# Re-orderings in a fused retention and snake-MLP kernel: a later cast, neighbouring value sets, other engines for squares, a first state and a sum, and swapped PSUM banks

## The chip, the core and the metric

The kernel runs on one core of a Trainium2 chip. The metric is the device time of one execution in microseconds (us); the median of the runs shown is compared. On the core five engines work beside each other, each through its own instruction stream in order: TensorE (PE in the profile, its weight loads PEld), VectorE (DVE), ScalarE (ACT), GpSimd (POOL) and SyncE (SP), which here only issues DMAs. They meet through semaphores: an instruction that waits holds up everything behind it on its own engine.

## The reference

Eight batches of causal retention (8 heads, 576 positions, head size 64), whose output is reshaped to 4608 tokens of 512 and goes through an MLP with a snake activation:

```python
scores = scale * np.matmul(q, k.transpose(0, 1, 3, 2))
Dmat = np.where(rel >= 0, gamma[:, None, None] ** rel[None, :, :], 0.0)
attn = np.matmul(scores * Dmat, v)                 # (8, 8, 576, 64)
x = attn.transpose(0, 2, 1, 3).reshape(8 * 576, 512)
h = x @ w_in                                       # (4608, 2048)
s = np.sin(alpha * h)
out = (h + s * s / (alpha + 1e-9)) @ w_out         # (4608, 512)
```

## The kernel before

**The retention.** The decay is folded into q and k when they are cast from float32 to float16 (`cast`, L138; the multiplication is L181; a v is only copied, by `copy`, L102 on ACT and L104 on DVE or POOL). A batch's first 512 positions are two blocks, `p` 0 and 1, of two chunks `g` each. Per block: `scores` (L348) multiplies k and q into a PSUM tile of two banks, `masked` (L366, the instruction is L370, on DVE) applies the causal mask and makes `ret`, and `values` (L379, matmul L401) multiplies `ret` with v. `outer` (L285, matmul L298) makes the sums of k times v per chunk; `take_sum`, `evict` and `evict_bank` copy them from PSUM to `kvs`; `more` (L336) carries the decayed sum on from chunk to chunk on POOL; `to_state` (L331, the instruction is L332) multiplies a chunk's sum by one decay factor per partition and head (`g1`, four columns) into a float16 state, one POOL instruction of 128x256. `add_states` (L412, matmul L423) adds state times q to the values, and `keep` (L430) casts the result to `xT`, the input of the MLP.

**Two value sets and their order.** The values of a block come in two sets, "not same" and "same", which use different halves of the array's rows on the same PSUM bank, so the second may begin only when the first is through. With `relay=engine` an empty instruction on that engine waits for the first set's last matmul, and the second set's first matmul waits for it (`told`, L248; `order`, L240). It stands in that engine's stream like any other instruction. Without a relay TensorE drains itself before the second set (`change_rows`, L234).

**The MLP.** 512 tokens are a block `n`; the 2048 columns of h are 16 units. `project(n, u, tag)` (L528, four matmuls L536 for all 512 columns, or four for each half) fills the bank `tag`; `sine` (L541, L544, ACT) reads it; `square` (L549; L553 on ACT, L555 on DVE or POOL) squares the sine; `product` (L558, L560, DVE) adds the scaled square to h, writes `gT` and so frees the bank. `gemm2(n, u, tag)` (L577, four matmuls L582) multiplies `gT` with w_out for blocks 0 and 1; `finish` (L571) evicts and stores. From block 2 on the second product is done with seven instead of eight quarter products (`Quarters`, L605): its sums `s1` to `s4` of parts of `gT` (L619 to L631) run on DVE or POOL, its matmuls are L653.

**What sets the order.** All of it is written out by hand: `tc.manual_schedule()` keeps each engine's instructions in the order of the calls. PSUM has eight banks under six names: `h0`, `h1`, `h2`, `op` of one bank, `m0`, `m1` of two. A call that takes a name waits until the last user of that bank has been read. Blocks 0 to 2 of the MLP are interleaved call by call with batches 1 to 4 of the retention; from block 3 on a loop over `n` does it. Loads go out on SP's queue, w_in and w_out on POOL's. Six raw buffers hold loaded q, k and v; a `load` waits until a buffer has been cast.

Around the change, before:

- Batch 0, L785 to L833: POOL casts the second block's q, ACT takes the transposes out of PSUM (`take`), POOL makes the first state (L803), and the second block's two value sets stand with `project(0, 0)` between them (L827 to L829), the relay on DVE.
- Units 0 to 3 of block 0, L840 to L855: squares on DVE, ACT, POOL, DVE.
- Block 1 with batch 2, L1029 to L1113. `at[2].outer` takes `op` and `h2`. On ACT the cast of the second half of batch 3's first v (L1076) stands between `sine(1, 12)` and `square(1, 12)`. The first value sets of both blocks (L1096, L1097) have a relay on DVE, with `product(1, 14)` and a cast behind; `gemm2(1, 4)` stands between first and second sets.
- Block 3, L1414: the sum `Q.s1(1)` on DVE after unit 10.

Of the kernel before, what the change touches and what calls it, by code (L numbers as in the profile page):

```python
# [18 lines left out]
def kernel(  # L19
# [16 lines left out]
    nc = tc.nc  # L36
# [37 lines left out]
    g1 = cn[:, 48:52]  # L74
# [13 lines left out]
    V, A_, G_ = nc.vector, nc.scalar, nc.gpsimd  # L88

    def load_w_in(g):  # L90
        cols = slice(g * 512, (g + 1) * 512)
        nc.gpsimd.dma_start(w_in16[:, :, cols], w_in_r[:, :, cols])
# [161 lines left out]
    class Attention:  # L254
# [76 lines left out]
        def to_state(self, c, eng=None):  # L331
            (eng or nc.gpsimd).tensor_tensor(  # L332
                self.state_of(c), self.kvs[:, c], g1.unsqueeze(2).to_broadcast([P, 4, D]), MULT
            )

        def more(self, c):  # L336
# [212 lines left out]
    def square(n, fc, eng):  # L549
        s_t = hps_of[n, fc][1]  # L550
        ss_t = work.tile([P, 512], F16, tag="ss", bufs=4, name="ss_t")
        if eng is nc.scalar:
            nc.scalar.activation(ss_t, s_t, mybir.ActivationFunctionType.Square)  # L553
        else:
            eng.tensor_tensor(ss_t, s_t, s_t, MULT)  # L555
        hps_of[n, fc][1] = ss_t
# [137 lines left out]
    def keep_busy(n, tag, m=512):  # L694
        idle = psum.tile([P, 512], F32, tag=tag, bufs=1, name="idle")
        for _ in range(n):
            matmul(idle[:, 0:m], zero[:, 0:P], zero[:, 0:m], start=True, stop=True)  # L697
# [43 lines left out]
    with tc.manual_schedule():  # L741
# [44 lines left out]
        cast(0, "q", 1, G_, (1,))  # L786
        load_w_in(2)
        keep_busy(5, "h2", 256)
        turn(0, "q", 1, "op", (0,))
# [12 lines left out]
        keep_busy(4, "h1", 256)  # L802
        at[0].to_state(0, G_)  # L803
        cast(0, "v", 1, G_, (0,))
# [21 lines left out]
        load_w_in(3)  # L826
        at[0].values(1, False, "m0", relay=V)  # L827
        project(0, 0, "op", 0)
        at[0].values(1, True)  # L829
        at[0].add_states(1, (0,))  # L830
        project(0, 1, "h2", 0)
        at[0].add_states(1, (1,))
        at[0].keep(1, A_)  # L833
        project(0, 2, "h0", 0)
        project(0, 3, "h1", 0)
# [7 lines left out]
        sine(0, 1)  # L843
        square(0, 1, A_)
        product(0, 0)
        project(0, 2, "h0", 1)
        sine(0, 2)
        square(0, 2, G_)
        product(0, 1)
        project(0, 3, "h1", 1)  # L850
        sine(0, 3)
        square(0, 3, V)
        product(0, 3)
        project(0, 4, "m1")
        product(0, 2)  # L855
        sine(0, 4)
# [171 lines left out]
        square(1, 6, A_)  # L1028
        at[2].outer((0, 1), "op", "h2")  # L1029
        at[2].evict_bank(1, V)  # L1030
        project(1, 7, "h0", 0)
        project(1, 7, "h0", 1)
        at[2].evict_bank(0, V)
        project(1, 8, "h1", 0)
        project(1, 8, "h1", 1)
        sine(1, 8)
# [8 lines left out]
        product(1, 8)  # L1045
        project(1, 10, "op", 0)
        project(1, 10, "op", 1)
        sine(1, 10)
# [12 lines left out]
        at[2].scores(0, 0, "m0")  # L1061
        gemm2(1, 0, "h1")
        sine(1, 9)
# [9 lines left out]
        project(1, 12, "h0", 1)  # L1073
        gemm2(1, 1, "h1")
        sine(1, 12)
        cast(3, "v", 0, A_, (1,))  # L1076
        square(1, 12, A_)
        product(1, 12)
        cast(3, "q", 1, G_)
        project(1, 13, "op", 0)  # L1080
        project(1, 13, "op", 1)
        gemm2(1, 2, "h1")
        at[2].scores(1, 0, "m0")
# [11 lines left out]
        square(1, 13, A_)  # L1095
        at[2].values(1, False, "m1", relay=V)  # L1096
        at[2].values(0, False, "m0", relay=V)  # L1097
        product(1, 14)
# [7 lines left out]
        cast(3, "q", 0, G_)  # L1106
        gemm2(1, 4, "h2")
        at[2].values(0, True)
# [3 lines left out]
        at[2].add_states(1)  # L1112
        at[2].keep(1, A_)  # L1113
        gemm2(1, 5, "h2")
        project(2, 3, "m0", 0)
# [27 lines left out]
        at[3].scores(1, 0, "m1")  # L1143
        gemm2(1, 3, "h1")
        project(2, 2, "op")
        project(2, 7, "h0")
# [11 lines left out]
        product(2, 7)  # L1158
        project(2, 11, "h1")
        gemm2(1, 12, "h2")  # L1160
# [9 lines left out]
        cast(4, "v", 1, A_)  # L1170
        project(2, 0, "op")
        at[3].masked(0, 1)
# [8 lines left out]
        sine(2, 0)  # L1181
        gemm2(1, 8, "h1")
        gemm2(1, 9, "h1")
        gemm2(1, 10, "h1")
        gemm2(1, 11, "h1")
        sine(2, 4)
        project(2, 8, "h0")
        cast(4, "q", 1, G_, (0,))
        project(2, 6, "op")
        cast(4, "k", 1, G_, (1,))  # L1190
# [4 lines left out]
        finish(1, 2)  # L1195
        at[4].outer((0, 1), "h2", "h1")
        cast(4, "q", 0, G_, (1,))
# [28 lines left out]
        sine(2, 5)  # L1226
        project(2, 15, "h1", 0)
        project(2, 15, "h1", 1)
        sine(2, 15)
# [4 lines left out]
        product(2, 15)  # L1234
        project(2, 13, "op", 0)
        project(2, 13, "op", 1)
        project(2, 14, "m0", 0)
# [42 lines left out]
        for n in range(3, NBLK):  # L1280
# [96 lines left out]
            if n == 3:  # L1377
                for x in KEYS[3:]:
                    cast(n + 2, *x, G_)
            if n == 6:  # L1380
                for j in range(3):
                    last_tokens(j, "cast")
                last_tokens(3, "load")
# [27 lines left out]
            if B2:  # L1411
                crossed(n + 2, 0, "k")
                crossed(n + 2, 1, "k")
            if n == 3:  # L1414
                Q.s1(1, V)
            if n == 8:
# [90 lines left out]
```

## Time and profile before

| | us |
|---|---|
| median of 3 runs | 299.24 |
| lowest, highest | 297.9, 300.09 |
| the profiled execution, its own time | 301.06 |
| its span, first to last instruction | 299.3 |
| TensorE busy in the span | 284.2 (95%) |
| VectorE busy | 220.2 (74%) |
| ScalarE busy | 209.7 (70%) |
| GpSimd busy | 207.1 (69%) |

The granted TensorE clock is 0.99 of full speed in the mean. A line of the timeline gives an instruction's start and duration in us, engine, source line, operation, the tile that it writes and those that it reads, and the count of instructions merged into it; in square brackets stands the idle time of the engine just before, and what ended it.

### The profile page before, as it was taken

How to read it: one execution, taken by the hardware profiler on the slowest of the kernel's cores; microseconds unless marked ns; L12 is line 12 of the kernel's file. 1: busy time of each engine (PE TensorE's matmuls, PEld its weight loads, DVE VectorE, ACT ScalarE, POOL GpSimd, SP SyncE). 2: the span in 40 equal slices, each digit the busy share in tenths (PEclk: the TensorE clock that was granted, in tenths of full speed). 3: DMA queues.
4: the chain of work that ended last, by engine and by line, in shares of the span. 5: the costliest groups of instructions: out<-in, count | busy, mean ns of one | idle time of the engine just before them, and what ended most of it. 6: DMA issues, size and time to landing. Idle time of an engine off the chain costs nothing.

```text
span 299.3 us, 8757 instructions
## 1 busy us (share of the span) xinstructions
PE 284.2 (95%) x3607; PEld 185.1 (62%) x3607; DVE 220.2 (74%) x299; ACT 209.7 (70%) x336; POOL 207.1 (69%) x200
## 2 busy tenths in 40 slices
PE   7798999997699999999999999999999999999993
PEld 5563454575354576666666666766666666665782
DVE  3849977886667899998778767786769485756871
ACT  2659832876376799787878787878777878887600
POOL 4876889999989787988897899779925900370000
PEclk9999999999799999999999999999999999999998
DMA  7999999998989297989699768676747201310225
GB/s 227 288 255 221 271 212 291 230 213 259 244 202 268 55 169 174 236 207 198 153 266 187 161 158 238 76 168 147 159 107 176 55 1 41 70 37 17 62 50 119
DMA packets 119159, 49.89 MB, mean 167 GB/s; under 512 B 69824, under 2 KB 118096, under 8 KB 119120
## 3 DMA queue, kind: packets, MB, share of 16 engines
q1 hardware_dynamic: 114528, 45.04, 64.0%
q0 software_dynamic: 4224, 4.19, 8.5%
q8 instruction: 28, 0.46, 0.7%
q10 hardware_dynamic: 368, 0.11, 0.2%
q14 instruction: 11, 0.09, 0.1%
HBM read 36.74 MB, written 9.44 MB: 154 GB/s over the span
## 4 chain that ended last, share of the span: by engine, by line
PE 82%; POOL 6%; ACT 4%; DVE 3%; DMA 2%; issue 2%; SPq 0%; ACTq 0%; DVEq 0%; POOLq 0%
PE hps L536 35%; PE hps L653 29%; PE ops L582 6%; POOL T L603 3%; PE sc L358 2%; DMA v<-in_v_dram 2%; PE o L401 2%; PE idle L697 2%; PE kv L298 2%; PE tr L215 1%; ACT s_t L544 1%; DVE ret L370 1%; DVE gT L560 1%; PE o L423 1%; POOL kvs L340 1%
## 5 line engine op out<-in xcount | busy, mean ns | idle before, releaser
L560 DVE SCALAR_TENSOR_TENSOR gT<-ss_t,inva,hps 128x512 f16<-128x512 f16 x144 | 105.8, 744 | 43.3 <-ACT ss_t L553 40.6
L536 PE MATMUL hps<-xT,w_in 128*128 128x512 f16 (+1 forms) x600 | 121.3, 348 | 3.1 <-DVE gT L560 1.9
L544 ACT ACTIVATE s_t<-hps,alpha_t 128x512 f16<-128x512 f32 x144 | 96.8, 681 | 36.0 <-PE hps L536 34.5
L536 PEld LDWEIGHTS <-w_in 128*128 128x128 f16 x664 | 63.4, 98 | 53.6 <-issue 4.0
L553 ACT ACTIVATE ss_t<-s_t 128x512 f16<-128x512 f16 x119 | 74.5, 630 | 3.4
L653 PEld LDWEIGHTS <-gT 128*128 128x128 f16 x656 | 63.8, 98 | 14.5
L625 POOL TENSOR_TENSOR gT<-gT,d 128x1024 f16<-128x1024 f16 x12 | 25.3, 2124 | 29.2 <-PE hps L653 28.5
L653 PE MATMUL hps<-T,gT 128*128 128x256 f16 x336 | 39.8, 273 | 0.0
L653 PE MATMUL hps<-w_out,gT 128*128 128x256 f16 x320 | 38.2, 273 | 0.0
L370 DVE TENSOR_TENSOR ret<-sc,mask 128x1024 f16<-128x1024 f32 (+1 forms) x32 | 35.0, 1118 | 2.7 <-PE sc L358 2.5
L673 DVE TENSOR_TENSOR osb<-osb,hps 128x512 f32<-128x512 f32 x35 | 24.0, 685 | 12.9 <-PE hps L653 11.7
L582 PE MATMUL ops<-w_out,gT 128*128 128x512 f16 x128 | 32.2, 387 | 1.0 <-DVE gT L560 1.0
L181 POOL TENSOR_TENSOR q<-q,cn 128x1024 f16<-128x1024 f32 (+1 forms) x16 | 25.9, 1634 | 0.2 <-DMA q<-in_q_dram 0.2
L631 POOL TENSOR_TENSOR gT<-gT 128x1024 f16<-128x1024 f16 x12 | 25.3, 2127 | 0.0
L102 ACT CAST xT<-o 128x1024 f16<-128x1024 f32 (+1 forms) x15 | 14.3, 960 | 11.7 <-PE o L423 11.7
L332 POOL TENSOR_TENSOR s<-kvs,cn 128x256 f16<-128x256 f32 x24 | 15.3, 641 | 10.1 <-ACT kvs L102 8.7
L340 POOL TENSOR_TENSOR kvs<-s,kvs 128x256 f32<-128x256 f32 x24 | 20.2, 841 | 2.4 <-ACT kvs L102 0.6
L582 PEld LDWEIGHTS <-gT 128*128 128x128 f16 x128 | 11.7, 99 | 13.7 <-issue 1.8
L181 POOL TENSOR_TENSOR k<-k,cn 128x1024 f16<-128x1024 f32 (+1 forms) x11 | 18.8, 1712 | 0.0
L339 POOL TENSOR_TENSOR s<-kvs,cn 128x256 f32<-128x256 f32 x24 | 17.1, 714 | 1.3 <-ACT kvs L102 1.1
L102 ACT COPY osb<-hps 128x512 f32<-128x512 f32 (+2 forms) x15 | 8.2, 549 | 13.5 <-PE hps L653 13.3
L555 DVE TENSOR_TENSOR ss_t<-s_t 128x512 f16<-128x512 f16 x19 | 12.5, 658 | 5.2 <-ACT s_t L544 5.1
(74 smaller groups left out, 272.5 us busy)
## 6 DMA issues: line engine op xcount, KB each, us to landing
out_dram<-osb SPq DMA_DIRECT2D x70, 128.0 KB, 2.5
q<-in_q_dram SPq DMA_DIRECT2D x16, 512.0 KB, 6.1
k<-in_k_dram SPq DMA_DIRECT2D x10, 512.0 KB, 8.4
v<-in_v_dram SPq DMA_DIRECT2D x10, 512.0 KB, 7.0
k<-in_k_dram SPq DMA_DIRECT2D x24, 128.0 KB, 3.7
v<-in_v_dram SPq DMA_DIRECT2D x24, 128.0 KB, 3.7
w_in<-in_moe_w_in_dram POOLq DMA_DIRECT2D x4, 512.0 KB, 9.3
w_out<-in_moe_w_out_dram POOLq DMA_DIRECT2D x4, 512.0 KB, 10.1
```

Of the source, the lines that this page charges most:

```text
L181: return eng.tensor_tensor(dst[:, a0:a1].rearrange("p a r t d -> p t (a r) d"), t_.rearrange("p (t a) x -> p t a x", t=2)[:, :, a0:a1].rea ...
L340: nc.gpsimd.tensor_tensor(self.kvs[:, c], s32, self.kvs[:, c], ADD)
L370: made = nc.vector.tensor_tensor(ret.rearrange("p t (z x) -> p (t z) x", z=2)[:, :, 0:n], sc.rearrange("p t (z x) -> p (t z) x", z=2)[:, : ...
L536: matmul(hps_of[n, fc][0][:, cols], w_in16[:, a, fc * P : (fc + 1) * P], xs[n][:, a, cols], start=(a == 0 and part != 1), stop=(a == KT - ...
L544: nc.scalar.activation(s_t, hps, mybir.ActivationFunctionType.Sin, bias=0.0, scale=alpha_t[:, fc : fc + 1],)
L553: nc.scalar.activation(ss_t, s_t, mybir.ActivationFunctionType.Square)
L560: nc.vector.scalar_tensor_tensor(gT[n][:, :, fc, :], ss_t.rearrange("p (t n) -> p t n", t=2), inva[:, fc : fc + 1], hps.rearrange("p (t n) ...
L582: matmul(ops[n, c, cols.start][:, cols], gT[n][:, c // 2, fk, c % 2 * P : c % 2 * P + P], w_out16[:, fk, cols], start=(fk == 0), stop=(fk ...
L625: eng.tensor_tensor(self.part(0, 0, i), self.part(1, 1, i), self.d3[:, 4 * i : 4 * i + 4], SUB)
L631: eng.tensor_tensor(out_, self.part(1, 0, i), self.part(0, 0, i), SUB)
L653: matmul(self.ps[name][:, 256 * m + cols.start : 256 * m + cols.stop], left(j)[:, P * m : P * m + P], right(j)[:, cols], start=(tag is not ...
L673: nc.vector.tensor_tensor(out_, a, self.ps[ps], ADD)
```

## The change

1. `cast(3, "v", 0, A_, (1,))` moves on ACT from behind `sine(1, 12)` to behind `square(1, 13)`.
2. Batch 2's value sets lose their relay, so TensorE drains itself between the first and second sets, and all four sets now stand next to each other, behind `product(1, 14)` and the casts of batch 3, and ahead of `gemm2(1, 4)`, which moves behind both `keep`s.
3. Batch 0's second block: the two value sets stand next to each other ahead of `project(0, 0)`, the relay is on ACT, and `project(0, 1)` moves behind `keep`.
4. Squares of units 0 to 3 of block 0: DVE, POOL, DVE, POOL (before DVE, ACT, POOL, DVE); `product(0, 2)` comes before `product(0, 3)`.
5. The first state of batch 0 is made by four ACT instructions of 128x64, one per column of `g1`, ahead of `turn(0, "q", 1)`; before it was one POOL instruction ahead of a v cast.
6. In block 1 the names `op` and `h1` are swapped from `at[2].outer` on, through `gemm2(1, 8)` to `(1, 11)`, `at[4].outer` and units 13 and 15 of block 2.
7. In block 3 `Q.s1(1)` moves from DVE, after unit 10, to POOL, between the casts of batch 5's two q.

```diff
+        def to_state_apart(self, c):
+            for a in range(4):
+                nc.scalar.mul(self.state_of(c)[:, a], self.kvs[:, c, a], g1[:, a : a + 1])
...
         load_w_in(2)
+        at[0].to_state_apart(0)
         keep_busy(5, "h2", 256)
         turn(0, "q", 1, "op", (0,))
...
         keep_busy(4, "h1", 256)
-        at[0].to_state(0, G_)
         cast(0, "v", 1, G_, (0,))
...
-        at[0].values(1, False, "m0", relay=V)
-        project(0, 0, "op", 0)
+        at[0].values(1, False, "m0", relay=A_)
         at[0].values(1, True)
         at[0].add_states(1, (0,))
-        project(0, 1, "h2", 0)
+        project(0, 0, "op", 0)
         at[0].add_states(1, (1,))
         at[0].keep(1, A_)
+        project(0, 1, "h2", 0)
...
-        square(0, 1, A_)
+        square(0, 1, G_)
...
-        square(0, 2, G_)
+        square(0, 2, V)
...
-        square(0, 3, V)
+        square(0, 3, G_)
+        product(0, 2)
+        project(0, 4, "m1")
         product(0, 3)
-        project(0, 4, "m1")
-        product(0, 2)
...
-        at[2].outer((0, 1), "op", "h2")
+        at[2].outer((0, 1), "h1", "h2")
...
-        project(1, 8, "h1", 0)
-        project(1, 8, "h1", 1)
+        project(1, 8, "op", 0)
+        project(1, 8, "op", 1)
...
         sine(1, 12)
-        cast(3, "v", 0, A_, (1,))
         square(1, 12, A_)
...
         square(1, 13, A_)
-        at[2].values(1, False, "m1", relay=V)
-        at[2].values(0, False, "m0", relay=V)
+        cast(3, "v", 0, A_, (1,))
         product(1, 14)
         cast(3, "k", 0, V, (0,))
...
         cast(3, "q", 0, G_)
-        gemm2(1, 4, "h2")
+        at[2].values(1, False, "m1")
+        at[2].values(0, False, "m0")
         at[2].values(0, True)
         at[2].values(1, True)
         at[2].add_states(0)
         at[2].keep(0, A_, V)
         at[2].add_states(1)
         at[2].keep(1, A_)
+        gemm2(1, 4, "h2")
         gemm2(1, 5, "h2")
...
                 for x in KEYS[3:]:
                     cast(n + 2, *x, G_)
+                    if x == ("q", 0):
+                        Q.s1(1, G_)
...
-            if n == 3:
-                Q.s1(1, V)
```

More of the change, by code (lines that the diff above doesn't have):

```diff
@@ L1045 @@
         product(1, 8)
-        project(1, 10, "op", 0)
-        project(1, 10, "op", 1)
+        project(1, 10, "h1", 0)
+        project(1, 10, "h1", 1)
         sine(1, 10)
@@ L1061 @@
         at[2].scores(0, 0, "m0")
-        gemm2(1, 0, "h1")
+        gemm2(1, 0, "op")
         sine(1, 9)
@@ L1073 @@
         project(1, 12, "h0", 1)
-        gemm2(1, 1, "h1")
+        gemm2(1, 1, "op")
         sine(1, 12)
-        cast(3, "v", 0, A_, (1,))
         square(1, 12, A_)
@@ L1079 @@
         cast(3, "q", 1, G_)
-        project(1, 13, "op", 0)
-        project(1, 13, "op", 1)
-        gemm2(1, 2, "h1")
+        project(1, 13, "h1", 0)
+        project(1, 13, "h1", 1)
+        gemm2(1, 2, "op")
         at[2].scores(1, 0, "m0")
@@ L1143 @@
         at[3].scores(1, 0, "m1")
-        gemm2(1, 3, "h1")
-        project(2, 2, "op")
+        gemm2(1, 3, "op")
+        project(2, 2, "h1")
         project(2, 7, "h0")
@@ L1158 @@
         product(2, 7)
-        project(2, 11, "h1")
+        project(2, 11, "op")
         gemm2(1, 12, "h2")
@@ L1170 @@
         cast(4, "v", 1, A_)
-        project(2, 0, "op")
+        project(2, 0, "h1")
         at[3].masked(0, 1)
@@ L1181 @@
         sine(2, 0)
[L1182 to L1185, printed above, removed]
+        gemm2(1, 8, "op")
+        gemm2(1, 9, "op")
+        gemm2(1, 10, "op")
+        gemm2(1, 11, "op")
         sine(2, 4)
@@ L1188 @@
         cast(4, "q", 1, G_, (0,))
-        project(2, 6, "op")
+        project(2, 6, "h1")
         cast(4, "k", 1, G_, (1,))
@@ L1195 @@
         finish(1, 2)
-        at[4].outer((0, 1), "h2", "h1")
+        at[4].outer((0, 1), "h2", "op")
         cast(4, "q", 0, G_, (1,))
@@ L1226 @@
         sine(2, 5)
-        project(2, 15, "h1", 0)
-        project(2, 15, "h1", 1)
+        project(2, 15, "op", 0)
+        project(2, 15, "op", 1)
         sine(2, 15)
@@ L1234 @@
         product(2, 15)
-        project(2, 13, "op", 0)
-        project(2, 13, "op", 1)
+        project(2, 13, "h1", 0)
+        project(2, 13, "h1", 1)
         project(2, 14, "m0", 0)
```

## The prediction

> **What bounds the kernel now.** I read the page first, then the chain of waits, a table of windows and the timelines of the places that the diff touches.
>
> ```profile
> span 299.3 us, 8757 instructions
> ...
> PE   7798999997699999999999999999999999999993
> ...
> PEclk9999999999799999999999999999999999999998
> ```
>
> The first row is the span; of the 40 slices, 7.48 us each, the second row gives TensorE's busy tenths and the third its granted clock. TensorE is the bound: behind the first four slices its row is full except at slices 10 and 11, 67 to 82 us, and in slice 11 the clock dips too. The chain of waits enters this hole through a load of v (start, length):
>
> ```profile
> 64.64 7.31 DMA v<-in_v_dram
> ```
>
> It is issued at 64.64 and waited for over 7.31 us. I cut this stretch and one of the start into windows of 3.41 us, the length for which the clock was down. The columns are the length, the busy time (and count) of PE, PEld, DVE, ACT and POOL, the granted clock, the DMA share and GB/s:
>
> ```profile
> 9.82:13.23 3.41, 2.44 (x35) 1.50 (x23) 3.36 (x4) 2.16 (x6) 2.86 (x4) 1.00 1.21 294
> 13.23:16.65 3.42, 2.86 (x126) 2.18 (x125) 3.42 (x4) 2.43 (x6) 3.26 (x6) 1.00 1.23 203
> ...
> 71.26:74.67 3.41, 1.83 (x31) 1.42 (x20) 1.46 (x2) 2.61 (x5) 3.25 (x5) 1.00 0.77 211
> 74.67:78.09 3.42, 1.15 (x37) 0.76 (x35) 2.49 (x4) 1.52 (x3) 3.42 (x5) 1.00 1.08 263
> 78.09:81.50 3.41, 3.41 (x61) 1.89 (x60) 2.09 (x1) 0.51 (x2) 3.41 (x3) 0.50 0.84 197
> ```
>
> After a window with 1.15 us of TensorE work the next ran at 0.50 of the clock. The instructions in the hole:
>
> ```profile
> 69.14 0.68 ACT L544 ACTIVATE s_t<-hps,alpha_t 128x512 f16<-128x512 f32 x1
> ...
> 71.39 1.05 PE L536 MATMUL hps<-xT,w_in 128*128 128x256 f16 x8
> ...
> 72.03 0.62 ACT L102 CAST v<-v 128x512 f16<-128x512 f32 x1 [2.21 <-DMA v<-in_v_dram]
> ...
> 72.55 0.62 ACT L553 ACTIVATE ss_t<-s_t 128x512 f16<-128x512 f16 x1
> ...
> 73.21 0.75 DVE L560 SCALAR_TENSOR_TENSOR gT<-ss_t,inva,hps 128x512 f16<-128x512 f16 x1 [2.98 <-ACT ss_t L553]
> ...
> 73.87 2.35 DVE L370 TENSOR_TENSOR ret<-sc,mask 128x1024 f16<-128x1024 f32 x2
> ...
> 74.01 1.03 PE L536 MATMUL hps<-xT,w_in 128*128 128x256 f16 x8 [1.57 <-DVE gT L560]
> ...
> 76.28 0.64 PE L401 MATMUL o<-ret,v 64*64 64x128 f16 x32 [1.23 <-DVE ret L370]
> ...
> 77.96 1.77 PE L582 MATMUL ops<-w_out,gT 128*128 128x512 f16 x4 [1.04 <-DVE gT L560]
> ...
> 82.35 1.03 PE L536 MATMUL hps<-xT,w_in 128*128 128x256 f16 x8
> ...
> 83.22 1.03 PE L582 MATMUL ops<-w_out,gT 128*128 128x512 f16 x4
> ...
> 84.18 0.71 PE L298 MATMUL kv<-v,k 64*64 64x64 f16 x64
> ```
>
> ACT stood 2.21 us in front of the cast of v, whose data had not landed, with square(1, 12) behind it. DVE's product waited for that square, both masked steps stood behind the product, and TensorE waited three times: 1.57, 1.23 and 1.04.
>
> **The hole, costed (items 1 and 2).** project(1, 14) ends at 71.39 + 1.05 = 72.44, and project(2, 3) starts at 82.35: 9.9 us. What work is that at full clock? A project in halves takes 83.22 − 82.35 = 0.87, a gemm2 84.18 − 83.22 = 0.96. The four value sets with states and drain are seen whole in batch 3, which has no relay already:
>
> ```profile
> 103.27 0.64 PE L401 MATMUL o<-ret,v 64*64 64x128 f16 x32
> ...
> 104.98 1.26 PE L536 MATMUL hps<-xT,w_in 128*128 128x512 f16 x6
> ```
>
> That is 104.98 − 103.27 = 1.7 us, the drain in it. So 0.87 + 1.7 + 2 × 0.96 = 4.5 of the 9.9 is work and 5.4 is lost. In the new order: square(1, 12) follows the sine at 69.14 + 0.68 = 69.8 and ends at 70.4, the product at 71.2, before project(1, 15) wants the bank at 72.4. The masked steps need scores that stand just before 71.39, so they run from 71.45 to 73.8. TensorE does project(1, 15) until 73.3, waits 0.5, does the value sets until 75.55 and both gemm2 until 77.5, where project(2, 3) can start: 4.85 earlier. The moved cast costs 0.62 behind square(1, 13), with v long landed; behind it on ACT stand batch 2's keeps, which gemm2(1, 4) and (1, 5) now cover. Without the relay no empty instruction stands in DVE's stream; before, product(1, 14) and the k cast were queued behind two of them.
>
> What is late next is DVE, and there POOL matters:
>
> ```profile
> 74.76 1.90 POOL L181 TENSOR_TENSOR q<-q,cn 128x1024 f16<-128x1024 f32 x1
> ...
> 77.73 1.90 POOL L181 TENSOR_TENSOR q<-q,cn 128x1024 f16<-128x1024 f32 x1
> ...
> 77.82 2.36 DVE L181 TENSOR_TENSOR k<-k,cn 128x512 f16<-128x512 f32 x1
> ...
> 82.22 0.68 DVE L181 TENSOR_TENSOR k<-k,cn 128x512 f16<-128x512 f32 x1
> ```
>
> The same k cast took 2.36 when it began just after POOL's q cast, and 0.68 otherwise. Newly it is ready at 73.8 + 0.75 = 74.55, 0.2 ahead of POOL's first q cast. If POOL comes first, DVE's cast ends at 76.66 + 0.68 = 77.35, keep at 78.0, and the second k cast falls behind the q cast that ends at 79.63: it ends at 80.3 against 82.9 before, and only 2.6 remain. Ends of the range: 2.6 and 4.85. I take 4.0, nearer the upper end, because DVE comes first by 0.2. The Trainium skill ("SBUF — State Buffer", section "Who interferes with whom") says that a DVE instruction with two SBUF inputs and a GpSimd one that reads SBUF exclude each other for a whole instruction, and the first comer wins. The trace agrees (2.36 against 0.68); by that rule, with DVE first, the hole would give 4.85 and the sum below 0.85 more.
>
> **The start (items 3 to 5).**
>
> ```profile
> 10.19 0.17 ACT L704 COPY alpha_t<-al_ps 128x16 f32<-128x16 f32 x1 [0.23 <-PE al_ps L701]
> ...
> 10.26 0.38 ACT L102 COPY kvs<-kv 128x256 f32<-128x256 f32 x1
> ...
> 11.18 0.59 ACT L102 COPY qT<-tr 128x512 f16<-128x512 f16 x1 [0.55 <-PE tr L215]
> ...
> 18.35 0.14 PEld L423 LDWEIGHTS <-s 64*64 64x64 f16 x8 [0.26 <-POOL s L332]
> ...
> 23.07 2.21 POOL L555 TENSOR_TENSOR ss_t<-s_t 128x512 f16<-128x512 f16 x2 [1.82 <-ACT s_t L544]
> ...
> 24.49 2.73 DVE L560 SCALAR_TENSOR_TENSOR gT<-ss_t,inva,hps 128x512 f16<-128x512 f16 x4
> ...
> 26.04 3.61 PE L536 MATMUL hps<-xT,w_in 128*128 128x512 f16 x16 [0.91 <-ACT s_t L544]
> ```
>
> The four ACT multiplications stand between 10.64 and the take at 11.18. No row shows one. Between 0.17 for 16 columns and 0.38 for 256, 64 columns come to 0.21; the upper bound is the 128x512 copy's 0.59. Four take 0.85 to 2.4, of which 0.55 fills idle time; the rest delays the transposes behind, and through them scores, masks and the second block's values: +0.3 to +1.8. Below nothing is possible: POOL loses an instruction, its later states come earlier, and the 0.26 that the weight load waited for a state may go, so −0.26 is the other end. I take +0.4, near the interpolation. By the Trainium skill ("ScalarE: Activation LUTs", sections "Rules for kernel authors" and "What ACT_TABLE_LOAD costs") multiplications belong on VectorE, and by its costs (186 ns, 93 more for a pointer operand, 0.833 per column, 93 of overlap) four take about 1.05 as an estimate, a delay of 0.5 instead of 0.4; no row here shows such an instruction.
>
> The neighbouring value sets cost a relay on ACT, which has just finished keep and next only keeps again. project(0, 0) fills TensorE later instead of earlier: 0.
>
> Squares: project(0, 8) at 26.04 stood idle 0.91 before it. It reuses the bank h0 of unit 2, whose product was second among the four from 24.49: 24.49 + 2 × 0.68 = 25.85. Without a square ACT's sines 2 and 3 come 0.6 earlier, the square of unit 2 is on DVE, and product(0, 2) is no longer behind product(0, 3): it is out by about 25.0. −0.9; other end 0, because a POOL square takes 1.1 where ACT's takes 0.62 and unit 1's product waits for it.
>
> **The bank swap (item 6).**
>
> ```profile
> 59.06 0.69 DVE L104 COPY osb<-ops 128x512 f32<-128x512 f32 x1
> ...
> 60.46 0.71 PE L298 MATMUL kv<-v,k 64*64 64x64 f16 x64 [0.29 <-DVE gT L560]
> ```
>
> outer waited 0.29 for product(1, 4), which freed `op` just before 60.46; `h1` is freed by the eviction at 59.06 + 0.69 = 59.75. So −0.3; project(1, 8), which now needs `op`, stands behind outer in any case. All later swaps exchange like for like.
>
> **s1 on POOL (item 7).**
>
> ```profile
> 116.75 2.12 POOL L625 TENSOR_TENSOR gT<-gT,d 128x1024 f16<-128x1024 f16 x1 [0.69 <-DVE d L619]
> ...
> 131.40 2.05 DVE L622 TENSOR_TENSOR gT<-gT 128x1024 f16<-128x1024 f16 x1
> ...
> 133.89 0.61 POOL L332 TENSOR_TENSOR s<-kvs,cn 128x256 f16<-128x256 f32 x1 [0.98 <-ACT kvs L102]
> ...
> 134.16 1.02 PE L536 MATMUL hps<-xT,w_in 128*128 128x512 f16 x4 [0.34 <-DVE gT L560]
> ```
>
> DVE loses 2.05 just ahead of a product for which TensorE waited 0.34: −0.3, other end 0. POOL takes on 2.1; 0.98 of idle time takes part, 1.1 delays batch 5's q cast, its transpose on SP and the states, which TensorE wants only in the next block. Without that cover it would cost 1.1.
>
> **Sum.** +0.4 + 0 − 0.9 − 0.3 − 4.0 − 0.3 = −5.1, against the profiled execution's 301.06 (span 299.3): 296.0. That execution lies 1.8 above the median of 299.24; carried to the median the sum gives 294.1. Best ends: −0.26 − 0.9 − 0.3 − 4.85 − 0.3 = −6.6, or 292.6.
>
> **The rivals.**
> A, the forecast: 294.1, chance 0.66.
> B, the ports decide: POOL's q casts come ahead of both k casts (2.6 left), the squares' POOL steps give back the 0.9, s1 gives 0. +0.4 − 0.3 − 2.6 = −2.5: 296.7. For it: POOL is busy 3.42 of 3.42 in 74.67:78.09, so it is always near. Against: 0.2 us of lead. Chance 0.15.
> C, the stall is partly this execution's: v took 7.31 to land, and the execution is 1.8 above the median. If it usually lands 1.6 sooner, ACT loses only 0.6, the hole is worth 4.0 − 1.6 = 2.4, and 0.7 if the half clock's 3.41 / 2 = 1.7 is absent as well. With 1.6, in the middle, the sum is −2.7: 296.5. Chance 0.10.
> D, the other side: the clock drops at the start. If each ACT multiplication takes 0.46 or more, TensorE loses 1.3 us in 9.82:13.23, whose 2.44 of work then falls to the 1.15 after which the clock was halved. The next window's 2.86 of work takes as much again: with +1.8 before it, +4.7. With the hole at its lower end and no other gain than outer's, −2.6 − 0.3, that is 301.0, and if the clock stays low for a second window, whose work is up to 3.4, 304. Against it: 54% (71.26:74.67) was not enough to halve it, and 72% has far to fall. Chance 0.09. The Trainium skill ("TensorE: Matmul & The Clock Gate", section "Why this matters for your kernels") allows pauses up to about 3 us; the trace differs, since 74.67:78.09 has none over 1.23 and was followed by half clock. By that rule D is impossible and its time would be A's.
>
> **The numbers.** Predicted 294.1. The range goes from the best ends, 292.6, to B and a little more, 297.5, and 0.5 further on each side for the scatter of the runs shown (297.9 to 300.09): 292.1 to 298.0. It holds A, B and C and leaves out D. About 1% (3 us, so 296.2 to 302.2 is "same") is what a measurement can tell. Faster: A's 0.66 and half of C and a sixth of B (by their spread), 0.73; same: the rest of B and C and half of D, 0.22; slower: 0.05.
>
> **What would show it.** Right: no wait of ACT for v; project(1, 15) starts right behind (1, 14); no window at 0.50 near 78; project(2, 3) 4 to 5 us earlier against project(1, 14) than before. Start: sine(0, 0) at 20.9 and project(0, 8) without a wait. Wrong: k casts of 2 us on DVE (B), a half-clock window before 20 us (D), or a POOL that TensorE waits for between 85 and 135 us.

## The result and the profile after

The kernel after takes 297.15 us in the median of 15 runs (295.83 to 298.39), the kernel before 299.24 beside it on the same chip (15 runs, 297.55 to 302.13). The ratio is 0.9929, with a 95% interval of 0.9906 to 0.9953: faster by 2.1 us (0.7%), where 5.1 were forecast. The medians are of all executions; the ratios leave out those that took over 1.5% more than the fastest of their kernel, such as two of the twelve of start_only below. The profiled execution of the kernel after took 295.89 us, with a span of 294.2: against the profiled execution before, 301.06, the whole forecast has come, in the median less than half of it. First the page of the kernel after, its span, TensorE's busy tenths and the granted clock:

```profile
span 294.2 us, 8759 instructions
...
PE   7799999999989999999999999999999999999993
...
PEclk9999999999999999999999999999999999999999
```

The hole of slices 10 and 11 is gone, and so is the dip of the clock. What is left is an 8 in slice 12, 81 to 88 us. The same stretch in the timeline of the kernel after (start, length, engine, line; from L336 on the line numbers are five higher than before):

```profile
69.92 0.64 PE L363 MATMUL sc<-qT,kT 64*64 64x128 f16 x32
...
70.49 1.92 PE L541 MATMUL hps<-xT,w_in 128*128 128x256 f16 x16
...
73.02 1.38 PE L406 MATMUL o<-ret,v 64*64 64x128 f16 x64 [0.61 <-DVE ret L375]
...
73.62 0.68 DVE L181 TENSOR_TENSOR k<-k,cn 128x512 f16<-128x512 f32 x1
...
74.49 0.62 ACT L102 CAST v<-v 128x512 f16<-128x512 f32 x1
...
76.23 0.95 DVE L181 TENSOR_TENSOR k<-k,cn 128x512 f16<-128x512 f32 x1
...
76.40 1.04 PE L541 MATMUL hps<-xT,w_in 128*128 128x256 f16 x8
...
80.20 0.64 PE L363 MATMUL sc<-qT,kT 64*64 64x128 f16 x32 [0.29 <-DMA qT<-q]
...
87.08 0.64 PE L363 MATMUL sc<-qT,kT 64*64 64x128 f16 x32 [0.95 <-DMA qT<-q]
```

The cast of v waits for nothing, project(1, 15) stands right behind project(1, 14) (the 16 matmuls from 70.49), the four value sets stand together after a wait of 0.61, DVE's k casts take 0.68 and 0.95, and project(2, 3) starts at 76.40 instead of 82.35. Before, it started 9.9 behind the end of project(1, 14); now 76.40 − (70.49 + 1.05) = 4.86. But the waits in the last two rows are new: TensorE now waits for batch 3's transposed q.

The start and the outer sums, in the timeline of the kernel after and, below it, the start of the kernel before:

```profile
8.89 0.64 PE L298 MATMUL kv<-v,k 64*64 64x64 f16 x32
...
10.52 1.06 ACT L339 ACTIVATE s<-kvs,cn 128x64 f16<-128x64 f32 x4
...
11.48 0.58 ACT L102 COPY qT<-tr 128x512 f16<-128x512 f16 x1
...
18.30 9.27 PE L541 MATMUL hps<-xT,w_in 128*128 128x256 f16 x56
...
20.32 3.72 ACT L549 ACTIVATE s_t<-hps,alpha_t 128x512 f16<-128x512 f32 x6 [0.89 <-PE hps L541]
...
27.99 1.02 PE L541 MATMUL hps<-xT,w_in 128*128 128x512 f16 x4 [0.42 <-DVE gT L565]
...
38.77 0.45 PE L298 MATMUL kv<-v,k 64*64 64x64 f16 x32
...
59.56 0.71 PE L298 MATMUL kv<-v,k 64*64 64x64 f16 x64
```

```profile
8.90 0.64 PE L298 MATMUL kv<-v,k 64*64 64x64 f16 x32
...
39.30 0.45 PE L298 MATMUL kv<-v,k 64*64 64x64 f16 x32
```

From the first to the third sums of k times v it takes 38.77 − 8.89 = 29.88 instead of 30.40: 0.5 less, the forecast's +0.4 − 0.9. project(0, 8) lies without a wait among the 56 matmuls from 18.30; a new wait of 0.42 stands three projects later, at 27.99. outer at 59.56 has no wait any more. The group of the projects on the page shows the rest, busy time, mean ns, and idle time ahead with its releaser:

```profile
L541 PE MATMUL hps<-xT,w_in 128*128 128x512 f16 (+1 forms) x600 | 121.1, 348 | 0.4 <-DVE gT L565 0.4
```

Of the waits for a product only the 0.42 at 27.99 is left; the one of 0.34 in block 3, which item 7 was to remove, is gone.

### The profile page after: what moved, and what is told of

Read it like the earlier page. It is cut to its first block, busy times and chain, and to the rows that moved or that the text cites. A ratio compares the mean times of both kernels' runs of the same rounds, so it can differ in the third digit from the quotient of the medians.

```text
span 294.2 us, 8759 instructions
## 1 busy us (share of the span) xinstructions
PE 281.9 (96%) x3607; PEld 184.4 (63%) x3607; DVE 217.9 (74%) x298; ACT 209.0 (71%) x339; POOL 210.1 (71%) x201
## 4 chain that ended last, share of the span: by engine, by line
PE 77%; POOL 8%; DMA 5%; DVE 4%; SPq 2%; ACT 2%; issue 1%; POOLq 0%; ACTq 0%
PE hps L541 35%; PE hps L658 29%; PE ops L587 4%; POOL T L608 4%; DMA q<-in_q_dram 4%; PE sc L363 2%; PE o L406 2%; SPq L121 2%; DMA qT<-q 1%; DVE gT L565 1%; PE kv L298 1%; POOL q L181 1%; DVE ret L375 1%; PE tr L215 1%; POOL v L104 1%
## 5 line engine op out<-in xcount | busy, mean ns | idle before, releaser
L678 DVE TENSOR_TENSOR osb<-osb,hps 128x512 f32<-128x512 f32 x35 | 23.9, 684 | 11.9 <-PE hps L658 11.3
L587 PE MATMUL ops<-w_out,gT 128*128 128x512 f16 x128 | 31.2, 380 | 0.0
L345 POOL TENSOR_TENSOR kvs<-s,kvs 128x256 f32<-128x256 f32 x24 | 19.1, 797 | 2.5 <-ACT kvs L102 0.8
L332 POOL TENSOR_TENSOR s<-kvs,cn 128x256 f16<-128x256 f32 x23 | 16.1, 703 | 4.1 <-ACT kvs L102 3.3
L560 DVE TENSOR_TENSOR ss_t<-s_t 128x512 f16<-128x512 f16 x19 | 13.4, 708 | 5.7 <-ACT s_t L549 5.6
L344 POOL TENSOR_TENSOR s<-kvs,cn 128x256 f32<-128x256 f32 x24 | 16.3, 678 | 0.2
```

Of the source, the lines that this page charges most:

```text
L587: matmul(ops[n, c, cols.start][:, cols], gT[n][:, c // 2, fk, c % 2 * P : c % 2 * P + P], w_out16[:, fk, cols], start=(fk == 0), stop=(fk ...
L678: nc.vector.tensor_tensor(out_, a, self.ps[ps], ADD)
```

## The experiments

The question: why does a trace that gives all that was forecast stand for a median that gives less than half? The first theory was that the profiled execution of the kernel before was not typical: the long wait for v and the half clock belong to some executions only (near rival C of the prediction). The second was that the gain is given back behind the hole.

I measure the hole by one stretch that all kernels have: from batch 2's last scores to batch 3's first (in the kernel after 80.20 − 69.92 = 10.28 us, in the kernel before 85.79 − 70.81 = 14.98), and what follows by the stretch from there to batch 3's second scores (6.88 after, 5.92 before).

### The kernel before, seven times

The kernel before unchanged: before_again is twelve executions, of which one is profiled (median 298.91); the others are one profiled execution each.

> The kernel before, unchanged, profiled a second time, with its scatter. Theory T1 (the first profile of before showed a hole at 72 to 82 us that is longer than in the median execution): the cast of v waits under 1 us for its data, or no window near 78 us runs at half clock, project(2, 3) starts 2 to 3 us less after the end of project(1, 14) than the 9.9 us seen, and the span lies near 297.5. Theory T2 (the hole is as long in every execution; it is the changed kernel that loses time again in the median execution): wait of 2 us and more for v, 9 to 10 us from project(1, 14) to project(2, 3), as before.

> The kernel before, a third look. T5 (the first profile was long because v landed late against TensorE's arrival AND a window near 78 us ran at half clock, which a third of the executions do): with a half-clock window in the hole the time is 300 us and more and scores to scores over the hole take 14 to 15 us; without one 298 to 299 us and 12 to 13 us.

> The kernel before, a fourth look: as for the third. Rival to T5: a slow execution (over 300 us) that has no half-clock window in the hole, or a fast one that has it.

> The kernel before once more, one profiled execution. Theory (most executions have a short stall): if it takes 297.8 to 298.6 us, no window is at half clock, ACT waits 0.6 us or less for v in front of the cast, and batch 2's last scores to batch 3's first scores take 12.2 us or less; if it takes over 300 us, a half-clock window stands near 78 us or before 30 us. Rival (the 2.2 us wait is the rule and the gain goes elsewhere): the wait is 2 us or more and the stretch 14 us or more, also in an execution of 298.6 us or less.

> As for the run before it: theory, 298.6 us or less goes with a wait for v of at most 0.6 us, a stretch of 12.2 us or less and no half-clock window; over 300 us goes with a half-clock window. Rival: a wait of 2 us or more and a stretch of 14 us or more whatever the time.

> As for the two runs before it: theory, 298.6 us or less goes with a wait for v of at most 0.6 us, a stretch of 12.2 us or less and no half-clock window; over 300 us goes with a half-clock window. Rival: a wait of 2 us or more and a stretch of 14 us or more whatever the time.

The timelines of two of them, before_again and then before_sixth:

```profile
71.98 0.62 ACT L102 CAST v<-v 128x512 f16<-128x512 f32 x1 [0.60 <-DMA v<-in_v_dram]
...
72.38 0.64 PE L358 MATMUL sc<-qT,kT 64*64 64x128 f16 x32
...
84.46 0.70 PE L358 MATMUL sc<-qT,kT 64*64 64x128 f16 x32
```

```profile
71.37 0.62 ACT L102 CAST v<-v 128x512 f16<-128x512 f32 x1
...
72.48 0.64 PE L358 MATMUL sc<-qT,kT 64*64 64x128 f16 x32
...
84.20 0.64 PE L358 MATMUL sc<-qT,kT 64*64 64x128 f16 x32 [0.27 <-DVE gT L560]
```

In the first ACT waits 0.60 for v and the stretch is 12.08; in the second it waits for nothing and the stretch is 11.72. The cast of v starts at almost the same time as in the first profile (71.98 and 71.37 against 72.03), but TensorE comes later (72.38 and 72.48 against 70.81). In before_third the windows around the hole (columns as in the prediction) are those of the first profile:

```profile
72.20:75.60 3.40, 2.29 (x37) 1.59 (x26) 1.99 (x3) 3.08 (x6) 3.24 (x5) 1.00 0.95 280
75.60:79.00 3.40, 1.29 (x35) 0.86 (x36) 2.47 (x3) 1.08 (x2) 3.40 (x5) 1.00 1.07 217
79.00:82.40 3.40, 3.40 (x61) 1.91 (x60) 1.08 (x3) 1.52 (x3) 3.40 (x3) 0.50 0.85 217
```

A window of 1.29 us of work, then half clock. All seven by the same rows, the last column from the granted clock of the windows:

| execution | own time | cast of v at | ACT's wait for it | last scores at | stretch | half clock in the hole |
|---|---|---|---|---|---|---|
| first profile | 301.06 | 72.03 | 2.21 | 70.81 | 14.98 | yes |
| before_third | 301.32 | 72.43 | 1.59 | 71.84 | 14.25 | yes |
| before_fifth | 301.67 | 71.68 | 1.46 | 71.22 | 15.19 | yes |
| before_fourth | 299.93 | 72.12 | 1.06 | 72.07 | 12.54 | no |
| before_again | 299.71 | 71.98 | 0.60 | 72.38 | 12.08 | no |
| before_seventh | 298.88 | 71.32 | 0.38 | 71.94 | 11.89 | no |
| before_sixth | 299.21 | 71.37 | 0 | 72.48 | 11.72 | no |

Three executions over 301 us have the half clock in the hole, the four others, down to 298.88, do not. In the six executions with a wait v lands between 71.2 and 72.4, 6.4 to 8.2 us after its issue where the chain of waits shows it; by and large, the earlier TensorE comes, the longer ACT waits. (before_fourth, before_sixth and before_seventh have a half-clock window in the first 13 us instead. That need not be what makes them late: before_again, without one, has its last scores at 72.38.) So the prediction's execution was the worst case by its wait and second by its stretch; four of the seven have 11.7 to 12.5. That is the first theory; that a wait of 2 us is the rule, the rival of the last three expectations, is refuted. The theories' times hold less well: none of the last three executions fell between 297.8 and 298.6, and before_fourth took 299.93 without a half clock in the hole, where 298 to 299 were expected.

### One part of the change at a time

after_again is the kernel after, unchanged. hole_only is before with items 1 and 2, cast_only with item 1, start_only with items 3 to 5; no_start is the kernel after without items 3 to 5. The core of cast_only and of hole_only (which has it too):

```diff
         sine(1, 12)
-        cast(3, "v", 0, A_, (1,))
         square(1, 12, A_)
...
         square(1, 13, A_)
+        cast(3, "v", 0, A_, (1,))
```

```diff
-        at[2].values(1, False, "m1", relay=V)
-        at[2].values(0, False, "m0", relay=V)
...
-        gemm2(1, 4, "h2")
+        at[2].values(1, False, "m1")
+        at[2].values(0, False, "m0")
         at[2].values(0, True)
...
         at[2].keep(1, A_)
+        gemm2(1, 4, "h2")
```

And of start_only:

```diff
+        at[0].to_state_apart(0)
...
-        at[0].to_state(0, G_)
...
-        square(0, 1, A_)
+        square(0, 1, G_)
...
-        square(0, 2, G_)
+        square(0, 2, V)
...
-        square(0, 3, V)
+        square(0, 3, G_)
```

> The changed kernel, unchanged, profiled a second time, with its scatter. T1: a span of 294 to 295.5, the stretch from project(1, 14) to project(2, 3) again 5 us, and the rest like the first profile within 0.5 us. T2: a span of 295.5 to 296.5 with a loss of 1 to 2 us in a place where the first profile had none: scores waiting for a transposed q near 80 or 87 us (0.29 and 0.95 there), or a half-clock window in the first 20 us.

> The kernel before with items 1 and 2 alone: the cast of v later, batch 2's value sets next to each other without a relay. T1 and the prediction's sum agree that this carries most of the gain: by the prediction -4.0 us in a profile, by T1 -1.5 to -2 us in the median (ratio 0.993 to 0.995). T2: -4 us in the part up to 83 us and a part of it lost behind, median ratio 0.990 to 0.995. A third theory T3, that the start gives the gain and the hole is not worth anything in the median: ratio 0.998 to 1.002.

> The kernel before with item 1 alone, the cast of v behind square(1, 13). T1: ACT no longer waits for v, the 1.57 us (first profile) or 0 to 0.9 us (later ones) before project(1, 15) go and nothing else: the values still wait for the masked steps and the relay on VectorE stays, so project(2, 3) comes 0.5 to 1.5 us nearer to project(1, 14); median ratio 0.996 to 0.999. The prediction's reading, that the cast's wait is what opens the whole hole: 3 us and more, ratio below 0.992.

> The kernel before with items 3, 4 and 5 alone: the second block's value sets next to each other, squares of units 0 to 3, the first state on ScalarE. By the prediction's sum -0.5 us (+0.4 - 0.9), ratio 0.998; T1 the same; T3: -1.5 to -2 us, ratio 0.993 to 0.995. If what is won by 30 us is lost in the wait for v, which ends when the data lands and not earlier, the ratio is 1.000.

> The changed kernel without items 3, 4 and 5 (items 1, 2, 6 and 7 alone). If the start gains 0.5 us, as the prediction's sum has it, and the later cast lets it through: 0.5 us slower than the changed kernel, ratio 0.994 to 0.996 to the kernel before. If the start is worth nothing in the median (start_only gave 1.0027): the same as the changed kernel, 0.992 to 0.994.

| kernel | median (runs) | ratio to before [95%] | stretch of the hole | next stretch |
|---|---|---|---|---|
| after_again | 296.99 (10) | 0.9949 [0.9927, 0.9971] | 9.93 | 6.64 |
| hole_only | 297.77 (12) | 0.9958 [0.9927, 0.9989] | 9.93 | 6.48 |
| cast_only | 298.13 (12) | 0.9967 [0.9936, 0.9998] | 11.73 | 5.86 |
| start_only | 299.76 (12) | 1.0027 [0.9996, 1.0058] | 13.04 | 5.92 |
| no_start | 297.79 (12) | 0.9949 [0.9924, 0.9974] | 10.63 | 5.86 |

The timeline of hole_only, from which its two stretches come:

```profile
70.72 0.64 PE L358 MATMUL sc<-qT,kT 64*64 64x128 f16 x32
...
80.65 0.70 PE L358 MATMUL sc<-qT,kT 64*64 64x128 f16 x32
...
87.13 0.64 PE L358 MATMUL sc<-qT,kT 64*64 64x128 f16 x32 [0.49 <-DMA qT<-q]
```

Items 1 and 2 make the stretch 9.93, 1.8 to 2.6 shorter than in an execution of before without the half clock, and by 5 us against the first profile's. Item 1 alone leaves 11.73: the wait is gone, and so is the half clock (none of the twelve profiled executions with the cast later or, below, the load earlier has one in the hole, three of the seven of before have), but it gains little on an execution that had neither. Its ratio of 0.9967 refutes the reading that the cast's wait opens the whole hole, 3 us and more. In the profiles item 2 is the other 1.8. In the medians it doesn't show: 0.9958 for hole_only against 0.9967 for cast_only, with overlapping intervals, and less than the 0.993 to 0.995 expected. Part of the reason stands in hole_only's own profile: its next stretch is 0.6 longer than cast_only's, and in block 3 TensorE waits 0.77 for a product instead of 0.35. In start_only, TensorE comes to the hole at 70.83, as early as in the first profile, and this happens:

```profile
70.83 0.64 PE L363 MATMUL sc<-qT,kT 64*64 64x128 f16 x32
...
71.39 0.62 ACT L102 CAST v<-v 128x512 f16<-128x512 f32 x1 [1.57 <-DMA v<-in_v_dram]
```

ACT waits 1.57 for v, the stretch of the hole is 13.04 instead of 11.7 to 12.5, and the kernel is not faster. That fits the reading that without item 1 what the start gives is lost before the landing of v; one profile and a median don't show that nothing else takes it. With item 1 it can count, but how much the medians don't settle (no_start 297.79 against 296.99 to 297.57 for the kernel after; the intervals overlap).

### The load of v earlier instead of its cast later

```diff
-        load(3, "q", 1)
         load(3, "v", 0)
+        load(3, "q", 1)
```

> The kernel before with batch 3's load of v issued one place earlier on SP's queue, ahead of its q. The cast of v stays where it was. T1 (the wait is for data that lands at a fixed time): the landing comes 1.5 to 2.5 us earlier, at about 70 us, the wait falls to under 0.5 us, and the time is that of cast_only within 0.5 us: ratio 0.996 to 0.999, with a q cast on GpSimd that has its data well before 74 us anyway. If the wait had another cause than the landing, it stays at 0.6 to 2.2 us and the ratio is 1.000.

The timeline of v_first:

```profile
70.14 0.61 ACT L102 CAST v<-v 128x512 f16<-128x512 f32 x1
```

v is there when ACT comes to the cast at 70.14, and ACT does not wait; the stretch is 11.74, next to cast_only's 11.73, and the ratio 0.9961 [0.9936, 0.9985] next to 0.9967. So it is the wait for v, and not the place of the cast in ACT's stream as such, that item 1 is worth.

### What is given back: two sets of loads

SP's queue in the kernel after, then the same queue and TensorE's second scores in loads_later (q and k are batch 4's, the transposes batch 3's):

```profile
78.13 0.58 SPq L121 DMA_DIRECT2D q<-in_q_dram  x1
...
78.76 0.56 SPq L121 DMA_DIRECT2D k<-in_k_dram  x1
...
79.42 3.10 SPq L205 DMA_TRANSPOSE kT<-k  x1
...
82.63 2.12 SPq L205 DMA_TRANSPOSE qT<-q  x1
```

```profile
79.90 1.26 SPq L205 DMA_TRANSPOSE kT<-k  x1
...
82.02 2.00 SPq L205 DMA_TRANSPOSE qT<-q  x1
...
84.07 0.58 SPq L121 DMA_DIRECT2D q<-in_q_dram  x1
...
88.34 0.64 PE L363 MATMUL sc<-qT,kT 64*64 64x128 f16 x32
```

In the kernel after the k transpose, issued 0.1 us behind two loads, holds the queue for 3.10 us; with the loads behind the transposes it is 1.26, and the second scores wait for nothing. A second such place is the last v of batch 4. The kernel before, then after_again:

```profile
98.91 1.03 ACT L102 CAST v<-v 128x1024 f16<-128x1024 f32 x1
```

```profile
97.52 1.04 ACT L102 CAST v<-v 128x1024 f16<-128x1024 f32 x1 [3.04 <-DMA v<-in_v_dram]
...
98.62 0.19 PE L298 MATMUL kv<-v,k 64*64 64x64 f16 x1 [0.32 <-ACT v L102]
...
99.10 0.70 PE L298 MATMUL kv<-v,k 64*64 64x64 f16 x63 [0.30 <-ACT osb L102]
```

ACT now waits 3.04 us for it (2.26, 2.17 and 2.12 in the other profiles of the kernel after), its load standing behind four stores, as before; in this one execution TensorE waits too. The edits, the first of loads_later (and loads_later_2, the same kernel), the second of v4_early, both together in both_later:

```diff
-        load(4, "q", 1)
-        load(4, "k", 0)
         cast(3, "v", 0, G_, (0,))
...
         crossed(3, 0, "q")
+        load(4, "q", 1)
+        load(4, "k", 0)
```

```diff
         load(4, "q", 0)
+        load(4, "v", 0)
         at[3].masked(1, 0)
         finish(1, 0)
         finish(1, 1)
...
         gemm2(1, 13, "h2")
-        load(4, "v", 0)
```

> The changed kernel with the loads of batch 4's second q and first k issued behind batch 3's last transposes instead of ahead of them. T4 (what the hole gave is partly given back because the transposed q of batch 3 lands behind those two loads): the wait of 0.3 to 1.0 us before scores near 87 us goes, and the median falls by 0.5 to 0.9 us against the changed kernel, ratio 0.990 to 0.992 to the kernel before. Rival: the q cast on GpSimd sets the transposes' time, then the wait stays and the ratio is that of the changed kernel; or batch 4's q, k, v land too late and a new wait of 1 us or more appears at 91 to 99 us, ratio above 0.994.

> The changed kernel with batch 4's first two loads behind batch 3's last transposes, again, beside the changed kernel. T4: no wait for the transposed q near 87 us and 0.4 to 0.8 us less than the changed kernel, ratio to the kernel before 0.990 to 0.992. Rival (the wait goes but comes back before 100 us, or lies under what the start scatters): the same as the changed kernel within 0.3 us.

> The changed kernel again, on the same chip as loads_later_2, to compare the two: 297.0 us, the ratio to the kernel before 0.993 to 0.995, no half-clock window between 70 and 90 us, and 0.5 to 1.0 us of waiting for the transposed q near 87 us.

> The kernel after with batch 4's last v load issued directly behind its q load, ahead of the four stores of finish(1, 0) and finish(1, 1). In the profiles of the kernel after, ACT waits 2.2 to 3.0 us for this v at 96 to 97 us (0 to 0.2 in the kernel before). Theory (this wait is a second place where the gain is given back, in some executions): the load is issued near 87.8 instead of 91.1, the wait falls below 0.5 us, TensorE has no pause at 98 us, from batch 3's second scores to the next scores it takes 23.9 us, and the median is 0.3 to 0.8 us below the kernel after's. Rival (TensorE does not depend on it): the stores land later, and the median is within 0.2 us of the kernel after's.

> The kernel after with both moves of loads: batch 4's first q and k behind batch 3's last transpose, and batch 4's last v ahead of the stores of finish(1, 0) and (1, 1). Theory: no wait of TensorE for the transposed q of batch 3 and none at 98 us; batch 3's first to second scores 6.1 us, second to next 23.9; median 0.6 to 1.2 us below the kernel after's, 295.9 to 296.4 where that lies at 297.0. Rival: the loads that start later let v land later, and the wait of ACT at 92 or 97 us comes back; median as the kernel after's.

> The kernel after, unchanged, beside the two runs before it on the same chip. Theory: a median near 297.0 as in the calls before, a wait of ACT of 2 to 3 us for batch 4's last v and one of TensorE of 0.6 to 1.0 us for batch 3's transposed q.

| kernel | median (runs) | ratio to before [95%] | stretch of the hole | next stretch |
|---|---|---|---|---|
| loads_later | 296.86 (7) | 0.992 [0.9888, 0.9952] | 9.92 | 6.09 |
| loads_later_2 | 296.69 (6) | 0.9899 [0.9853, 0.9946] | 9.93 | 5.99 |
| after_third (beside loads_later_2) | 297.01 (10) | 0.992 [0.9886, 0.9954] | 9.92 | 6.63 |
| v4_early | 296.63 (6) | 0.9885 [0.9847, 0.9924] | 10.10 | 6.80 |
| both_later | 296.46 (6) | 0.9878 [0.9842, 0.9914] | 10.18 | 5.86 |
| after_fourth (beside the two above) | 297.57 (11) | 0.9941 [0.9904, 0.9977] | 9.93 | 7.23 |

Each edit removes the wait that it aims at: the next stretch falls to 5.9 to 6.1 where the loads come later, and in v4_early the last v is cast at 94.13 without a wait. Against the kernel after measured beside them the medians are 0.3, 0.9 and 1.1 lower (loads_later_2, v4_early, both_later), but the intervals overlap, and the 0.3 is nearer to the rival of loads_later_2 than to its theory. What v4_early gains is not explained by its wait: in three of the four profiles of the kernel after that wait costs TensorE nothing (from batch 3's second scores to the next scores it takes 23.82 to 23.89, next to 23.88 in v4_early and 23.93 to 23.95 in the kernel before; only after_again has 24.98). In both_later, the fastest version seen, another wait comes in their place (its timeline):

```profile
86.07 0.64 PE L363 MATMUL sc<-qT,kT 64*64 64x128 f16 x32
...
91.73 1.05 ACT L102 CAST v<-v 128x1024 f16<-128x1024 f32 x1 [1.71 <-DMA v<-in_v_dram]
...
110.98 0.64 PE L363 MATMUL sc<-qT,kT 64*64 64x128 f16 x32
```

ACT waits 1.71 for batch 4's first v, and from the second scores to the next it takes 24.91, where 23.9 were expected and the kernel after's first profile shows 23.89 (87.08 to 110.97). So part of what the later loads give is taken back by a later v, as its rival said, and the theory that the two gains add up holds only in part. From batch 3's first scores over the second to the next, loads_later, loads_later_2 and both_later take 30.43 to 30.77, the kernel after 30.45 to 31.62, the kernel before 29.78 to 30.03: in the traces most of the wait moves and does not go.

## Why the prediction was wrong

The direction was right, and so was the mechanism of the hole: in the profiled pair the signs came that the prediction named for it. The size was wrong. **The step that failed is "the hole, costed", and with it "carried to the median".** The new order was priced well: project(2, 3) was to start 9.9 − 4.85 = 5.05 behind project(1, 14), and starts 4.86 behind it. What does not hold is the old length. The −4.0 was worked out as "9.9 of which 5.4 is lost" in an execution in which ACT waited 2.21 for v and the clock was halved behind it; in the four executions without that half clock the same 9.9 are 6.3 to 7.5 (with project(1, 14) taken as 1.05). The prediction then took off the 1.8 by which this execution was above the median as if it lay anywhere. It lay in the hole: those four have 11.7 to 12.5 in the stretch between the scores instead of 14.98. And the sum has no term for what comes back behind the hole.

The profiles give, as an estimate for an execution without a half clock in the stretch concerned: hole 12.0 to 9.9 (middle of four each), −2.1 where the sum had −4.0; the next stretch 5.92 to 6.8, +0.8 where it had nothing; start −0.9; outer 0; s1 −0.3. That is −2.5 beside the measured −2.1.

- **Start (items 3 to 5).** Forecast +0.4 − 0.9, and −0.5 in the first pair of profiles. Over all profiles without a half clock there, the first to the third sums take 30.40 to 31.00 (eight executions, middle 30.78) without these items and 29.86 to 30.64 (six, middle 29.87) with them: −0.9. The row of the four ACT multiplications is 1.06 (0.27 each; 0.21 was taken), and the take behind them came 0.3 later (11.48 against 11.18). The estimate from the Trainium skill ("ScalarE: Activation LUTs", section "What ACT_TABLE_LOAD costs") was 1.05, nearer than the interpolation; the trace agrees. sine(0, 0) came at 20.32 (20.9 forecast); of the 0.91 in front of project(0, 8) half came back three projects later. start_only suggests that before item 1 such a gain does not pass the landing of v, which the prediction did not consider.
- **Item 6 and item 7.** Both waits, 0.29 and 0.34, are gone, as forecast. But the 0.29 stands in none of the six other executions of before, so in most there was nothing for item 6 to gain; the wait of item 7, 0.30 to 0.39, stands in all seven.
- **Rival B** (ports) did not come: the k casts on DVE took 0.68 to 1.06 in the four profiles of the kernel after, and in all of them DVE's first k cast began before POOL's q cast. So in the first pair of profiles, where the stretch of the hole fell by 4.7, the upper end, 4.85, was nearer than the 4.0 taken.
- **Rival C** (the stall partly this execution's) is what happened, but not for its reason. v does not usually land sooner: it landed at 64.64 + 7.31 = 71.95 here and between 71.2 and 72.4 in the others, and 7.31 us is not long for this load. It was TensorE that came early. That its price, 296.5, lies only 0.65 below the measured time is therefore partly luck: it took 2.4 off the hole and still carried the 1.8. It had a chance of 0.10, although the 1.8 above the median was a sign that the prediction named itself.
- **Rival D** (half clock at the start): not by the ACT multiplications, but the clock is halved there in some executions of both kernels; below.
- **What is late next**: the prediction named DVE and POOL. In the next stretch it was DMA: batch 3's transposes behind batch 4's loads; ACT then waits for batch 4's last v, which costs TensorE time in one of four profiles. TensorE came earlier, but batch 4's first two loads did not (78.13 on SP's queue against 77.97).

## What to carry to other kernels

A stall seen in one profile is a sample: where it waits for a transfer that lands at its own time, and a clock dip stands behind it, price it on several executions, and ask whether the distance of the profiled execution from the median lies in that very stall. When a stall in the middle is removed, list the loads behind it that are issued by the hand-written order: what TensorE gains is worth only what the next transfers can follow. A gain ahead of a transfer that lands at its own time can turn into a longer wait for it; remove that wait first.

## What the runs showed of the hardware

How little work makes the clock drop is not a fixed share here. Windows of 3.40 us, cut so that they meet the edges of a half-clock stretch of the same execution (the last pair by counting on from 12.70 in steps of 3.41, the length of a half-clock stretch), in after_third and in before_sixth:

```profile
18.50:21.90 3.40, 1.65 (x26) 1.10 (x26) 0.77 (x3) 0.53 (x2) 3.22 (x6) 1.00 1.17 292
21.90:25.30 3.40, 3.40 (x19) 2.42 (x16) 0.04 (x1) 1.26 (x2) 2.01 (x3) 0.50 1.19 303
```

```profile
5.90:9.30 3.40, 2.04 (x25) 1.55 (x26) 2.58 (x5) 2.17 (x4) 0.77 (x1) 1.00 1.15 345
9.30:12.70 3.40, 3.35 (x74) 2.62 (x72) 2.61 (x3) 0.83 (x4) 3.33 (x5) 0.50 1.18 312
...
74.10:77.50 3.40, 1.72 (x42) 1.21 (x40) 2.47 (x4) 2.99 (x5) 3.24 (x5) 1.00 0.96 199
77.50:80.90 3.40, 3.18 (x69) 1.85 (x68) 2.46 (x3) 1.85 (x3) 3.40 (x4) 1.00 0.52 82
```

1.65 us of TensorE work in 3.40 was followed by half clock, 1.72 was not; but 2.04, earlier in before_sixth, was. No pause in these windows was longer than 1.3 us, so a bound on the pause alone, as in the Trainium skill ("TensorE: Matmul & The Clock Gate", section "Why this matters for your kernels"), does not cover them. What decides between 1.65 and 2.04 the runs don't settle. The half clock does not begin at the same place of the program in every execution: it began 7.3, 7.2 and 4.7 us behind batch 2's last scores in the first profile, before_third and before_fifth. So the same hole can halve the clock once and not the next time. This would fit the scatter of the kernel before, from 297.55 to 302.13; it was not shown for each execution. The kernel after has such executions too: after_third's profiled one, in which v came late at the start and the clock was halved from 21.90, took 300.30.
